# Soft-MoE slot work of three batches deferred to the last two head pairs, and chunk bounds from three products

## The chip, the core and the metric

The kernel runs on one core of a Trainium2 chip. The metric is the device time of one execution in microseconds (us). A core has five engines with queues of their own: TensorE (PE in the profile; PEld is its weight load), VectorE (DVE), ScalarE (ACT), GpSimd (POOL) and SyncE (SP). Each works off its own queue in the order in which the program wrote it; semaphores order the engines among each other. SBUF is the working memory, PSUM holds what TensorE writes. The loads are issued from GpSimd's queue, the stores from SyncE's.

## What is computed

Causal attention over selected key chunks, followed by a soft mixture of experts. Batch 4, heads 8, sequence 768, head dimension 64, key chunks of 32.

```python
# attention: each query keeps the 6 chunks with the largest upper bound
k_min, k_max = min and max of k over each chunk of 32 keys
ub = sum_d max(q * k_min, q * k_max)          # (B, H, S, 24), causal chunks only
sel = the 6 chunks of largest ub
scores = q k^T / 8, masked to sel and causal; attn = softmax(scores); x = attn v
# soft MoE on x as (3072, 512) with phi (512, 32), 8 experts of 4 slots, F = 1024
logits = x @ phi
d = softmax of logits over the 3072 rows      # dispatch, one column per slot
slot_input = d.T @ x                          # (32, 512)
slot_out[e] = relu(slot_input[e] @ w1[e]) @ w2[e]
c = softmax of logits over the 32 slots       # combine
out = c @ slot_out                            # (3072, 512)
```

## The kernel before

**Pairs.** The work runs over 16 pairs of heads, four per batch (pair 0 to 15; the text calls the loop step i "pair i"). Each step of the loop handles several pairs at different stages: the scores and exponentials of pair i, the bound and the search of pair i+1, the transposes of k and q of pair i+2, the products with v of pair i-1, the normalisation of pair i-2. Loads run four pairs ahead. The order of the work on each engine is the order in which the loop writes it; nothing reorders it.

**Scores.** `GROUPS` packs the causal blocks of a pair into six score groups of 384 or 512 columns. Each goes into one of two PSUM buffers (pool `p_sc`), is read by one ScalarE exponential (line 293, tile e_sb), and its diagonal blocks are cut by a GpSimd select (line 295). Between groups 1 and 2 the loop puts the bound products and the transposes of k, and the first half of the products with v; between groups 3 and 4 the transposes of q and more products with v.

**Bounds and search.** `evac_T` copies the transposed k and q to SBUF on ScalarE (line 190). `kmin` and `kmax` reduce k over chunks on VectorE, `qsplit` makes min(q,0) and max(q,0) (lines 215 and 216), and `ubound` forms the bound as min(q,0) k_min + max(q,0) k_max: one causal product (line 222) and twelve products of 128 x 48 (line 229). `select` runs twelve maximum-of-eight searches (line 241) and compares with the sixth largest (line 244). `ns_transposes` and `evac_ns` bring the result to the mask that is added to the scores.

**Slots.** When the four pairs of a batch are normalised and transposed, its slot work follows: `moe_logits` and `moe_copy` (copy and column maximum pm) at the end of the step i with i - 2 the last pair of the batch, that is i = 5, 9 and 13; and in the next step (6, 10 and 14) `moe_max`, `moe_bound`, `moe_exp` (running column maximum m_run, dispatch exponential d_sb, rescaling of the sum so far), `moe_comb` (row maximum, combine exponentials into the padded tile c_pad), `moe_dispatch` (30 small products into si, added to si_acc) and `moe_ct` (six transposes of c_pad and a copy into cT_all). The last batch does the same after the loop, in code of its own. The tag "tp" of pool `p_tp` has two PSUM buffers that all transposes, bounds and slot sums share.

**Experts.** After the loop: `experts_in` (x w1), `relu`, `hidden_T`, `experts_out` (w2), then 24 products with c and the stores. The 16 weight pieces of 1024 KB (pieces 0 to 7 are w1, 8 to 15 w2) are loaded along the loop. `EARLY` = 14 of them have tiles of their own; pieces 14 and 15 get theirs at the start of steps 14 and 15, in space that closed input pools leave. `wplan` says how many pieces a step issues:

```python
wplan = {i: 1 for i in range(-1, NPAIR)}
for i in (0, 1):
    wplan[i] = 0
```

`keep` issues idle products after the loop; their results are not used.

## Time and profile before

| | |
|---|---|
| device time, median of 3 runs | 173.73 us (173.69 to 173.76) |
| span of the profiled execution (first to last instruction) | 172.0 us; its device time is not listed apart, so the 1.7 us around the span are taken from the median |
| TensorE busy | 137.7 us (80%), 2574 products |
| VectorE busy | 126.0 us (73%), 429 instructions |
| ScalarE busy | 122.2 us (71%), 163 instructions |
| GpSimd busy | 99.7 us (58%), 192 instructions |
| on the chain that ended last | PE 37%, ACT 27%, DVE 17%, DMA 8%, issue 7% |
| loads through GpSimd's queue | 26.25 MB written to SBUF |
| stores | 6.29 MB |

The shares of busy time are averages over stages with different limits, so the page alone does not say what bounds. The chain that ended last is followed back from the last instruction, at each step to what released it. "issue" is time in which an engine waited for nothing that the profile shows. A row of the chain or of a timeline gives start, length, engine, tile or line, and how many instructions were merged. A row of the stages gives the stretch, its length, the busy time of PE, PEld, DVE, ACT and POOL with their instruction counts, the granted clock of TensorE, the DMA share and GB/s. A group row gives the line, engine, operation, out<-in, count, then busy us and mean ns of one, then the idle time ahead of it and who ended it.

### The profile page before, as it was taken

How to read it: one execution, taken by the hardware profiler on the slowest of the kernel's cores; microseconds unless marked ns; L12 is line 12 of the kernel's file. 1: busy time of each engine (PE TensorE's matmuls, PEld its weight loads, DVE VectorE, ACT ScalarE, POOL GpSimd, SP SyncE). 2: the span in 40 equal slices, each digit the busy share in tenths (PEclk: the TensorE clock that was granted, in tenths of full speed). 3: DMA queues.
4: the chain of work that ended last, by engine and by line, in shares of the span. 5: the costliest groups of instructions: out<-in, count | busy, mean ns of one | idle time of the engine just before them, and what ended most of it. 6: DMA issues, size and time to landing. Idle time of an engine off the chain costs nothing.

```text
span 172.0 us, 6181 instructions
## 1 busy us (share of the span) xinstructions
PE 137.7 (80%) x2574; PEld 99.3 (58%) x2575; DVE 126.0 (73%) x429; ACT 122.2 (71%) x163; POOL 99.7 (58%) x192
## 2 busy tenths in 40 slices
PE   0458988999999789999988899999697989896310
PEld 0345465776767658766675676676565854774200
DVE  3468768999999988999997989999843652156530
ACT  2355999999999679899977799998567621265430
POOL 7977759789878666889774678558253710000000
PEclk9999999999999999999999999999999999999955
DMA  3999999999999999999999999999999950019995
GB/s 46 169 145 188 184 213 187 130 159 210 171 203 194 210 198 206 198 205 201 204 202 200 206 197 209 195 211 198 202 210 213 215 107 0 4 37 402 403 406 221
DMA packets 40460, 32.94 MB, mean 191 GB/s; under 512 B 26352, under 2 KB 34544, under 8 KB 40432
## 3 DMA queue, kind: packets, MB, share of 16 engines
q0 software_dynamic: 38416, 26.25, 103.2%
q1 hardware_dynamic: 2016, 6.29, 9.3%
q8 instruction: 20, 0.33, 0.7%
q14 instruction: 8, 0.07, 0.1%
HBM read 52.49 MB, written 6.29 MB: 342 GB/s over the span
## 4 chain that ended last, share of the span: by engine, by line
PE 37%; ACT 27%; DVE 17%; DMA 8%; issue 7%; POOL 0%; ACTq 0%; DVEq 0%; POOLq 0%
ACT e_sb L293 20%; PE sc_ps L270 7%; DMA out_dram<-o_sb 6%; PE tr_ps L181 5%; PE at_ps L314 5%; PE sc_ps L280 4%; DVE x_sb L327 3%; PE h_ps L654 2%; PE so_ps L694 2%; DVE qpn L216 2%; PE ub_ps L229 2%; DMA k_in<-in_k_dram 2%; ACT kT L190 2%; DVE mm L199 2%; DVE mm L205 2%
## 5 line engine op out<-in xcount | busy, mean ns | idle before, releaser
L293 ACT ACTIVATE e_sb<-sc_ps 128x768 bf16<-128x768 f32 (+1 forms) x96 | 82.7, 927 | 7.0 <-PE sc_ps L280 6.5
L295 POOL TENSOR_SCALAR_AFFINE_SELECT e_sb<-e_sb 128x256 bf16<-128x256 bf16 x96 | 39.2, 415 | 25.6 <-ACT e_sb L293 25.3
L270 PE MATMUL sc_ps<-qT,kT 64*128 64x384 bf16 (+3 forms) x288 | 40.2, 297 | 6.6 <-ACT e_sb L293 6.5
L280 PE MATMUL sc_ps<-nsT,smask 64*128 64x384 bf16 (+2 forms) x320 | 38.7, 281 | 0.0
L314 PE MATMUL at_ps<-v_t,e_sb 128*128 128x65 bf16 x672 | 29.8, 194 | 1.8 <-DVE x_sb L327 1.6
L270 PEld LDWEIGHTS <-kT 64*128 64x128 bf16 x288 | 17.3, 95 | 18.3 <-issue 13.2
L314 PEld LDWEIGHTS <-e_sb 128*128 128x128 bf16 x672 | 25.2, 98 | 4.2 <-issue 1.5
L241 DVE MAX8 mx<-ub_ps 128x8 f32<-128x8 f32 (+1 forms) x192 | 17.0, 162 | 3.4 <-POOL e_sb L295 1.9
L280 PEld LDWEIGHTS <-smask 64*128 64x128 bf16 x320 | 16.7, 96 | 3.6 <-issue 0.6
L190 ACT COPY kT<-tr_ps 128x768 bf16<-128x768 bf16 x16 | 12.8, 798 | 8.2 <-PE tr_ps L181 7.1
L199 DVE TENSOR_REDUCE mm<-kT 128x24 bf16<-128x768 bf16 x16 | 15.1, 944 | 4.1 <-ACT kT L190 4.0
L134 POOL DMA_DIRECT2D v_t<-in_v_dram x16 | 16.6, 1041 | 2.0 <-PE ns_ps L252 1.3
L327 DVE TENSOR_TENSOR x_sb<-at_ps,inv 128x768 bf16<-128x768 f32 (+1 forms) x17 | 15.5, 910 | 0.6
L205 DVE TENSOR_REDUCE mm<-kT 128x24 bf16<-128x768 bf16 x16 | 15.1, 943 | 0.0
L190 ACT COPY qT<-tr_ps 128x768 bf16<-128x768 bf16 x16 | 12.9, 805 | 2.1 <-PE tr_ps L181 2.1
L181 PE MATMUL tr_ps<-ident,k_in 128*64 128x128 bf16 x192 | 9.4, 240 | 5.6 <-DMA k_in<-in_k_dram 4.8
L129 POOL DMA_DIRECT2D k_in<-in_k_dram x16 | 11.7, 729 | 1.5 <-POOLq L760 0.8
L740 ACT ACTIVATE o_sb<-o_ps,cinv 128x512 f32<-128x512 f32 x12 | 8.1, 686 | 5.6 <-DMA out_dram<-o_sb 4.3
L129 POOL DMA_DIRECT2D q_in<-in_q_dram x16 | 11.5, 720 | 0.0
L216 DVE TENSOR_SCALAR qpn<-qT 128x768 bf16<-128x768 bf16 x16 | 11.5, 716 | 0.0
L122 POOL DMA_DIRECT2D w_sb<-in_moe_w_dram x16 | 11.3, 708 | 0.0
L738 DVE TENSOR_SCALAR o_sb<-o_ps,cinv 128x512 f32<-128x512 f32 x11 | 8.0, 748 | 4.3 <-DMA out_dram<-o_sb 3.1
(116 smaller groups left out, 195.5 us busy)
## 6 DMA issues: line engine op xcount, KB each, us to landing
w_sb<-in_moe_w_dram POOLq DMA_DIRECT2D x16, 1024.0 KB, 13.4
out_dram<-o_sb SPq DMA_DIRECT2D x10, 512.0 KB, 5.4
k_in<-in_k_dram POOLq DMA_DIRECT2D x16, 192.0 KB, 9.6
q_in<-in_q_dram POOLq DMA_DIRECT2D x16, 192.0 KB, 9.6
v_t<-in_v_dram POOLq DMA_DIRECT2D x16, 192.0 KB, 10.1
out_dram<-o_sb SPq DMA_DIRECT2D x4, 256.0 KB, 3.3
phi_sb<-in_moe_phi_dram POOLq DMA_DIRECT2D x1, 32.0 KB, 8.8
```

Source lines behind the costliest of these rows:

```text
L129: nc.gpsimd.dma_start(out=t, in_=src.rearrange("h (p g) d -> p h (g d)", p=P))
L181: nc.tensor.matmul(ps[h * 64:(h + 1) * 64, g, :], lhsT=src[:, h, g * D:(g + 1) * D], rhs=ident, is_transpose=True,)
L190: nc.scalar.copy(t.rearrange("d (p g) -> d p g", g=NQT), st.pop((nm + "ps", i)).rearrange("d g p -> d p g"),)
L199: nc.vector.tensor_reduce(mm[:, 0, 0, :], kT, axis=AX.X, op=ALU.min)
L205: nc.vector.tensor_reduce(mm[:, 1, 0, :], kT, axis=AX.X, op=ALU.max)
L241: nc.vector.max(mx[:, a, :], ub[:, a, :max(8, 4 * t + 4)])
L270: nc.tensor.matmul(ps[:, h, c:c + w], lhsT=kT[r, kg * P:(kg + 1) * P], rhs=qT[r, qs], start=True, stop=False,)
L280: nc.tensor.matmul(ps[:, h, c + (f - t0) * P:c + (l - t0) * P], lhsT=smask[r, x, kg].rearrange("p a b -> p (a b)"), rhs=nsT[r, (f - x * NJ ...
L293: nc.scalar.activation(e[:, :, :w], st.pop(("scps", i, g))[:, :, :w], func=ACT.Exp, scale=scale)
L295: nc.gpsimd.affine_select(out=e[:, :, :P], in_=e[:, :, :P], compare_op=ALU.is_ge, fill=0.0, base=0, pattern=[[0, 2], [1, P]], channel_mult ...
L314: nc.tensor.matmul(o, lhsT=st["e", i, g][:, h, c:c + P], rhs=v_t[i % NV][:, h, kg, :], start=(kg == 0), stop=(kg == t),)
L327: nc.vector.tensor_tensor(st["x", b][:, t0:t1, 2 * j:2 * j + 2, :].rearrange("p t h d -> p h t d"), at[:, :, :, :D], inv.broadcast_to([P, ...
```

## The change

**Deferred slots.** Batches 0 to 2 do only the logits and the copy at i = 5, 9 and 13, into a tile lg_all that holds all three; their normalised x stays in SBUF (pool xo, three buffers). At the end of step 13 one reduction (`old_max`) takes the column maximum over the three batches. Step 14 does the transpose of that maximum, the shift, the exponential and the combine part for all 18 row blocks at once; step 15 and the code after the loop do the joint dispatch (18 products for each of five column groups) and the transposes of c.

**Bounds.** q is stored as -q, k_min as -k_min. The bound is (-q)(-k_min) + max(q,0)(k_max - k_min), by three products of the same shape in each row block: 18 for 12. The exponential takes the scale -1/8, and the mask changes its sign. `qsplit` is one VectorE instruction. Row block 0 has four chunks at most, so all are kept: it gets one maximum over four chunks and a threshold of -3e38 set once, and no search.

**Weights.** EARLY is 12. No piece is issued in steps 0, 1, 4 and 8, two in step 12. Pieces 12 to 15 are issued by `late_weight` once a pool closes: in step 13, in step 14 behind the search, after the loop, and behind the last products with v.

```diff
-    EARLY = 14
+    EARLY = 12
+    OLD = B - 1
+    NO = OLD * NQT
...
-        nc.scalar.copy(
+        nc.scalar.activation(
             t.rearrange("d (p g) -> d p g", g=NQT),
             st.pop((nm + "ps", i)).rearrange("d g p -> d p g"),
+            func=ACT.Copy, scale=-1.0 if nm == "q" else 1.0,
         )
...
-        nc.vector.tensor_scalar_min(t[:, 0, :], qT, 0.0)
-        nc.vector.tensor_scalar_max(t[:, 1, :], qT, 0.0)
+        nc.vector.tensor_scalar(t, st["qT", i], -1.0, 0.0, op0=ALU.mult, op1=ALU.max)
...
-            for x in range(2):
+            for z, (w, x) in enumerate(((qT, 0), (qp, 0), (qp, 1))):
                 nc.tensor.matmul(
-                    o, lhsT=qpn[:, x, t * P:(t + 1) * P],
-                    rhs=bd[:, x],
-                    start=False, stop=(t == NQT - 1 and x == 1),
+                    o, lhsT=w[:, t * P:(t + 1) * P], rhs=bd[:, x],
+                    start=False, stop=(t == NQT - 1 and z == 2),
                 )
...
+        nc.vector.tensor_reduce(mx[:, 0:3:2, 0:1], ub[:, 0:3:2, :4], axis=AX.X, op=ALU.max)
         for a in range(NQT * 2):
             t = a // 4 + NJ * (a % 2)
-            nc.vector.max(mx[:, a, :], ub[:, a, :max(8, 4 * t + 4)])
+            if t > 0:
+                nc.vector.max(mx[:, a, :], ub[:, a, :4 * t + 4])
...
     def moe_copy(b):
-        lg = small.tile([P, NQT, NS], F32, name="lg", tag="lg")
+        nc.vector.tensor_copy(lg_all[:, b], st.pop(("lgps", b)))
...
+    def old_max():
+        nc.vector.tensor_reduce(pm, lgo.rearrange("p n s -> p s n"), axis=AX.X, op=ALU.max)
+    def old_maxT():
+        nc.tensor.matmul(pmT, lhsT=st.pop("pm"), rhs=identf, is_transpose=True)
+    def old_bound():
+        nc.vector.tensor_reduce(mb, st.pop("pmT"), axis=AX.X, op=ALU.max)
+    def old_shift():
+        ... bc, m_run, ld = lgo - m_run over [P, NO, NS]
+    def old_exp():
+        nc.scalar.activation(d_o, st.pop("ld"), func=ACT.Exp)
+    def old_rows():
+        nc.vector.tensor_reduce(rm, lgo, axis=AX.X, op=ALU.max)
+        nc.vector.tensor_tensor(lgo, lgo, rm.broadcast_to([P, NO, NS]), op=ALU.subtract)
+    def old_comb():
+        ... two exponentials of lgo into c_pad [P, NO, 4, CH]
+    def old_dispatch(dgs):
+        ... 18 products for each dg of dgs; with the last dg a copy into si_acc
...
-    wplan = {i: 1 for i in range(-1, NPAIR)}
-    for i in (0, 1):
-        wplan[i] = 0
+    wplan = {i: 1 for i in (-1, 2, 3, 5, 6, 7, 9, 10, 11)}
+    wplan[12] = 2
```

In the loop (`LAST` is 15) the new calls stand at these places; behind each the engines that it uses:

```
step 13: ... moe_copy(2), old_max (DVE)
step 14: scores 0, 1 | old_maxT (PE) | ubound(15), normalise(12) | old_bound (DVE) | select(15) | late_weight
         pv(13) first half | old_shift (PE, DVE) | scores 2, 3 | old_exp (ACT) | x_transposes, evac_x | old_rows (DVE)
         scores 4, 5 | old_comb (ACT) | ns_transposes, evac_ns, rest of pv(13)
step 15: scores 0, 1 | moe_ct(0) (PE, DVE) | normalise(13) | pv(14) first half | old_dispatch([0]) (PE) | scores 2, 3
         x_transposes, pv(14) | old_dispatch([1, 2]) | scores 4, pv(14), scores 5
after:   late_weight | moe_ct(1) | old_dispatch([3, 4]), copy (DVE) | normalise(14), pv(15), x_transposes(14) ...
         moe_ct(2) with a ScalarE copy in the place of keep(2) | i_ctx.close(), late_weight | memsets, tail as before
```

More of the change, by code (lines that the diff above doesn't have):

```diff
@@ L84 @@
     cT_all = static.tile([P, B * NQT, P], BF16, name="cT_all")
-    c_pad = static.tile([P, NQT, 4, CH], BF16, name="c_pad")
+    c_pad = static.tile([P, NO, 4, CH], BF16, name="c_pad")
+    lg_all = static.tile([P, OLD, NQT, NS], F32, name="lg_all")
     si_acc = static.tile([P, NDG + 1, NS], F32, name="si_acc")
-    m_run = [static.tile([P, NS], F32, name=f"m_run{i}") for i in range(2)]
+    m_run = static.tile([P, NS], F32, name="m_run")
     w_sb = []
@@ L147 @@
     nc.vector.memset(ones_sq, 1.0)
+    for t in mx_t:
+        nc.vector.memset(t, -3e38)
     for t in v_t:
@@ L393, in moe_exp @@
         nc.vector.tensor_tensor(
[L394 removed]
+            ld, lgo, m_run.rearrange("p (o s) -> p o s", o=1).broadcast_to([P, NO, NS]), op=ALU.subtract,
         )
[L396 to L404 removed]
@@ L438, in moe_ct @@
+                    rhs=d_sb[:, k, :], start=(k == 0), stop=(k == n - 1),
+                )
+    def old_dispatch(dgs):
+        if 0 in dgs:
+            st["si_o"] = p_tp.tile([P, NDG + 1, NS], F32, name="si_ps", tag="tp")
+        dispatch(st["si_o"], st["d_o"], [(st["x", b], t) for b in range(OLD) for t in range(NQT)], dgs)
+        if NDG in dgs:
+            nc.vector.tensor_copy(si_acc, st.pop("si_o"))
+    def moe_ct(b, copy=nc.vector.tensor_copy):
         ps = p_tp.tile([P, NQT, P], BF16, name="cT_ps", tag="tp")
@@ L580 @@
     evac_x(LAST, 3, NQT)
-    keep(2)
+    moe_ct(2, nc.scalar.copy)
     moe_logits(BL, range(NDG - 1, NDG), lg1)
+    i_ctx.close()
+    late_weight()
+    pads = ctx.enter_context(tc.tile_pool(name="pads", bufs=1))
+    siT_pad = pads.tile([P, NDG, E, CH], BF16, name="siT_pad")
+    hT_pad = pads.tile([P, NFG, E, CH], BF16, name="hT_pad")
     nc.gpsimd.memset(siT_pad, 0.0)
     nc.gpsimd.memset(hT_pad, 0.0)
-    i_ctx.close()
     tail = ctx.enter_context(tc.tile_pool(name="tail", bufs=1))
-    m_old = m_run[(BL + 1) % 2]
+    m_old = m_run
     pm = small.tile([P, NS], F32, name="pm", tag="pm")
@@ L621 @@
     keep(1)
-    moe_dispatch(BL)
+    si = p_tp.tile([P, NDG + 1, NS], F32, name="si_ps", tag="tp")
+    dispatch(si, d_sb, [(st["x", BL], t) for t in range(NQT)], range(NDG + 1))
     op = ctx.enter_context(tc.tile_pool(name="op", bufs=5))
-    si = st.pop("si")
     zrow = tail.tile([1, 4, CH], F32, name="zrow")
```

158 lines of the change are left out of this document (71 added, 87 removed).

## Prediction

> **What bounds the kernel now.** I read the span and the DMA strip first, then the chain that ended last, then the busy time by stages, and last the timelines of TensorE and VectorE at the places that the chain names.
>
> ```profile
> core 0 of [0], span 172.0 us
> DMA  3999999999999999999999999999999950019995
> ```
>
> The sum below is made on this span. The median of the three runs is 173.73 us, so 1.7 us lie around the span; they are added at the end unchanged. The DMA engines are busy for the first 33 of 40 slices: the loads are a second bound that lies close behind the first, and they come back among the rivals.
>
> The chain, over one ordinary pair:
>
> ```profile
> 41.32 1.77 ACT e_sb L293 x2
> 43.86 0.30 PE ub_ps L229 x12
> 44.16 0.46 PE tr_ps L181 x12
> 44.61 0.48 PE at_ps L314 x12
> 45.10 0.32 PE sc_ps L270 x2
> 45.68 0.45 ACT e_sb L293
> ```
>
> An ordinary pair is one closed ring. ScalarE works off its exponentials; the last of them frees a score buffer; TensorE then does the second score group of the next pair, the bound products (ub_ps), the transposes of k, the first products with v and the third score group, in this order; and ScalarE goes on only when that group is done (45.68). VectorE and GpSimd do not appear. Whatever is added to TensorE between 43.1 and 45.7 lengthens every pair; whatever is taken from VectorE in an ordinary pair gains nothing.
>
> The stages, from the start of one third exponential to a later one (columns: stretch, its length, then the engines' busy times):
>
> ```profile
> 45.68:52.55 6.87, 6.55 (x132) 4.73 (x128) 6.46 (x23) 6.53 (x9) 5.75 (x12) 1.00 1.19 193
> 52.55:69.71 17.16, 15.26 (x321) 11.69 (x316) 15.40 (x54) 13.72 (x19) 11.62 (x22) 1.00 1.34 202
> 83.45:101.06 17.61, 15.34 (x321) 11.80 (x316) 15.56 (x56) 13.89 (x20) 11.66 (x23) 1.00 1.32 202
> 114.80:123.65 8.85, 8.09 (x163) 6.06 (x157) 8.06 (x29) 6.16 (x9) 5.06 (x10) 1.00 1.31 203
> 123.65:131.21 7.56, 5.12 (x111) 3.97 (x111) 3.86 (x9) 5.39 (x9) 3.10 (x7) 1.00 1.24 208
> 131.21:136.43 5.22, 5.01 (x111) 3.78 (x106) 2.41 (x5) 4.57 (x5) 2.43 (x5) 1.00 1.07 216
> ```
>
> An ordinary pair takes 6.87 us. The two pairs that carry the slot work of batch 0 take 17.16 us, 3.42 more than two ordinary ones; batch 1 costs 17.61 - 13.74 = 3.87. Batch 2 is in the fourth and fifth row. Only there is the slot work on the path, and there it is a relay of small VectorE, TensorE and ScalarE steps:
>
> ```profile
> 119.50 0.48 DVE pm L365
> 120.15 0.72 DVE x_sb L327
> 121.29 0.97 DVE mx L241 x12
> 122.28 0.46 DVE ns_t L244
> 122.87 0.37 DVE ld L393
> 123.75 1.83 ACT e_sb L293 x2
> ```
>
> The exponential of the slots (d_sb) stands in ScalarE's queue ahead of the third score group, so that group waits for ld behind the whole search. A pair later it goes on so:
>
> ```profile
> 126.82 0.74 PE si_ps L426 x30
> 127.56 0.40 PE at_ps L314 x12
> 127.96 0.35 PE cT_ps L440 x6
> 128.33 0.56 DVE cT_all L443
> 129.06 0.97 DVE x_sb L327
> 130.08 0.55 PE at_ps L314 x12
> ```
>
> Thirty products of the dispatch take 0.74 us, 25 ns each; six transposes of c and their copy to SBUF follow, and only then the normalisation (x_sb) that releases the products with v.
>
> **The change, part by part.**
>
> *Three bound products for two (adds).* Six more weight loads and products in each pair, between second and third score group, on the ring.
>
> ```profile
> 43.70 0.46 PE L229 MATMUL ub_ps<-bd,qpn 128*128 128x48 bf16 x12
> 44.09 0.53 PE L181 MATMUL tr_ps<-ident,k_in 128*64 128x128 bf16 x12
> ```
>
> Twelve go from 43.70 to 44.09, that is 33 ns each; six more cost 0.20 us. Thirteen such passes lie ahead of the third exponential of pair 13 (114.80): 13 x 0.20 = +2.5 us. Nothing hides it. Lower bound: the 25 ns of the narrower dispatch products, +1.9; upper bound within the ring: the 12 transposes at 0.46/12 = 38 ns, +3.0. I take 33, which is the same operation. The Trainium skill (TensorE: Matmul & The Clock Gate, Back-to-back issue gap) speaks against this part: it gives about 81 ns as the sustained spacing of weight load and product at 128 columns. By that the thirteen passes would cost 6.3 us and the sum would end at +2.2 us; the trace's 33 ns for 48 columns do not agree with it.
>
> *q split, search and copies (removes, mostly free).* One VectorE pass makes max(q,0) where two made min and max; one small maximum over four chunks replaces two searches of row block 0; k and q are evacuated by an activation with a scale in the place of a copy, of the same size on the same engine. In ordinary pairs VectorE is off the ring: nothing. At the start it is on it:
>
> ```profile
> 8.92 0.79 DVE qpn L216
> ```
> ```profile
> 15.80 0.62 PE ub_ps L229 x11
> ```
>
> The first pair waits 0.79 us for the second pass of the split, and this one goes. But the products run slower there (0.62/11 = 56 ns), so two passes of six more cost 0.67 of it back where they are exposed, and behind the split the smask copy on ScalarE is next. I take -0.3 us, between -0.8 and +0.3. The longer memset of the padded c tile lies before the first k arrives.
>
> *Batches 0 and 1 (moves).* Pairs 5, 6, 9 and 10 keep only the logits and one copy on VectorE:
>
> ```profile
> 55.97 0.75 PE L356 MATMUL lg_ps<-phi_sb,xT_sb 128*128 128x32 bf16 x24
> ```
>
> These 0.75 us fall mostly into TensorE's wait for the last exponential; the copy fits into VectorE, which is freed of the second split pass and of pm. So of 3.42 + 3.87 = 7.29 us I leave 0.2 per batch: -6.9. Bounds: nothing left (-7.3), or the logits and a copy fully exposed, 1.0 a batch (-5.3).
>
> *Window of pair 13 to 14.* The joint maximum runs over 576 values where pm ran over 192. VectorE's price per element is (0.97 - 0.40)/576 = 1.0 ns, from x_sb (768 values, above) and lc (192):
>
> ```profile
> L412 DVE TENSOR_TENSOR lc<-lg,rm 128x192 f32<-128x192 f32 x3 | 1.2, 396 | 0.1
> L397 ACT ACTIVATE d_sb<-ld 128x192 bf16<-128x192 f32 x3 | 1.1, 363 | 4.2 <-DVE ld L393 4.2
> L393 DVE TENSOR_TENSOR ld<-lg,m_run 128x192 f32<-128x192 f32 x3 | 1.1, 357 | 0.1
> L410 DVE TENSOR_REDUCE rm<-lg 128x6 f32<-128x192 f32 x3 | 1.0, 346 | 0.0
> ```
> ```profile
> L415 ACT ACTIVATE c_pad<-lc 128x96 bf16<-128x96 f32 x6 | 1.4, 278 | 1.3 <-DVE lc L412 1.3
> ```
>
> So the maximum takes 0.48 + 0.38 = 0.86, and normalise behind it ends 0.2 to 0.4 us later than at 121.1 (120.15 + 0.97), the lower if the shorter q split lets it begin earlier. But the joint exponential is queued behind the third and fourth score groups, so these no longer wait for search and ld: 121.3 + 0.48 (products with v) + 0.3 (the broadcast, an estimate at the size of the 0.35 for six transposes) + 0.6 (scores) = 122.7, where it was 123.7. I take -0.85; from -1.4 (maximum hidden) to +0.4 (the broadcast waits for VectorE's queue).
>
> *Window of pair 14 to 15.* ScalarE gets 0.36 + 0.34 = 0.70 for the joint exponential (0.9 ns an element from the two activations above) and 0.9 for two of 288 in the place of 0.46; ld, row maxima and their subtraction are 0.74, 0.73 and 0.78 on VectorE beside it. Of what followed on the path (126.82 to 130.08), the 30 products leave (-0.74); the transposes of batch 0 and their copy take the place of batch 2's, but now wait for the c exponentials; 18 products of the joint dispatch (25 ns each, 0.45) stand ahead of the third score group. Sum +0.70 + 0.44 + 0.45 - 0.74 = +0.85, and 0.15 for the wait: +1.0, from +0.3 to +1.8.
>
> *From there to the last logits.* TensorE is busy 5.01 of 5.22 us, so what is added counts: 36 products ahead of the fifth score group, 0.90; transposes of batch 1, 0.37; 36 more products, 0.90; and now normalise of pair 14 stands in VectorE's queue behind the copy of their sum (0.35) instead of beside the scores, of which I count 0.4 more. Sum +2.9; from +1.5 (products fill waits) to +4.4 (both c copies and the sum's copy in series). Batch 2's transposes replace the two idle keep products: nothing. The late weights are cover that may go, below.
>
> Sum: +2.5 - 0.3 - 6.9 - 0.85 + 1.0 + 2.9 = -1.65 us. Span 170.4, time **172.1 us**.
>
> **The rivals.**
>
> *The join costs more (slower).* Place: pairs 14, 15 and the end, where hardly an engine has slack. With the upper bounds of the last three terms (+0.4, +1.8, +4.4) the sum is +1.9, 175.6 us; it turns slower once the three exceed the 4.7 us that the other terms save. For it: three steps are single-file through VectorE and the one bound buffer of the joint sum. Against it: before, VectorE was busy only 2.41 of 5.22 us there. Middle of the part of this case that is slower: 174.8.
>
> *The join hides (faster).* Lower bounds of the last two terms (+0.3, +1.5): -3.75, 170.0 us. For it: ScalarE and VectorE idle in 123.65 to 131.21. Against it: the DVE queue's order is fixed.
>
> *The last weight piece comes late.* It is now issued only when the last products with v are done. These with v end where the sixth row of the stages ends, 136.43; less the 1.65 of the sum it is issued near 134.8. It is needed by the products at
>
> ```profile
> 147.97 1.89 PE so_ps L694 x64
> ```
>
> shifted to 146.3. So 11.5 us are left:
>
> ```profile
> DMA to landing us min/median/max: 9.4/13.4/18.3
> ```
>
> At the median it stalls 1.9 us (174.0, no difference that can be told); slower from 13.6 us on; at the maximum 178.9. Against it: only one other piece is ahead in the queue by then, so I expect the minimum, 144.2.
>
> *The deferral doesn't free the pairs.* If logits, copy and their buffer are the excess, 1.0 a batch stays: 173.7.
>
> *Products at the early spacing of 56 ns.* At six times 56 ns, 0.34 a pair, the thirteen passes cost 4.4 in the place of 2.5: +0.25, 174.0, and any dearer is slower. Only the first pairs show this spacing. By the spacing that the Trainium skill gives (TensorE: Matmul & The Clock Gate, Back-to-back issue gap) it would be 175.9.
>
> **How the numbers follow.** A measurement of this kernel tells 0.2%, 0.35 us, from no change. Forecast 0.57 (172.1; own range 170.8 to 173.3); join hides 0.12; join costs more 0.13; late weight 0.08 (0.03 same, 0.05 slower); not freed 0.06 (0.04 same, 0.02 slower); products dearer 0.04 (slower). Faster: 0.54 + 0.12 = 0.66. Same: 0.03 (the upper end of the forecast) + 0.03 + 0.04 = 0.10. Slower: 0.13 + 0.05 + 0.02 + 0.04 = 0.24. The range 170.0 to 174.8 takes the hiding join and the middle of the costly one in; the late weight at its worst and the costlier half of the join stay out.
>
> **What would show it.** Ordinary pairs at 7.07 us with 18 bound products in 0.6 us; VectorE's share of an ordinary pair down by 0.6 or more; pairs 5, 6, 9 and 10 within 0.3 us of the ordinary ones; the third exponential of pair 13 near 110; the first logits of the last batch near 134.8; no wait of the expert products for a DMA. Ordinary pairs above 7.2 us, more than 4 us added after pair 13, or so_ps waiting for a weight load would prove it wrong.

## The result, and the profile after

| | before | after |
|---|---|---|
| device time, median | 173.74 us | 172.26 us (172.09 to 173.58) |
| ratio, 95% interval | | 0.994 (0.9917 to 0.9963) |
| profiled execution: time, span | span 172.0 us | 173.2 us, span 171.5 us |
| VectorE busy in the span | 126.0 us, 429 instructions | 114.9 us, 380 instructions |
| TensorE products | 2574 | 2663 |

The change gains 0.6% (1 - 0.994; the ratio is taken over all single times, the quotient of the two medians is 0.9915). 172.1 us was forecast. One thing is needed to read the numbers: the times of the changed kernel lie in two groups, 172.1 to 172.3 us with a mean granted TensorE clock of 0.961 to 0.970, and 173.2 to 173.6 us with 0.953 to 0.955, and the profiled execution is one of the second group.

```profile
core 0: 171.5 us, clock 0.954
```

The stages of the changed kernel, cut as in the prediction (stretch, length, busy PE, PEld, DVE, ACT, POOL with counts, granted clock, DMA share, GB/s): an ordinary pair, the pairs of batch 0 and of batch 1, the window of pair 13 to 14, that of pair 14 to 15, and from there to the last batch's first logits.

```profile
37.92:44.95 7.03, 6.71 (x138) 4.89 (x134) 5.83 (x22) 6.54 (x9) 5.82 (x12) 1.00 1.22 191
51.96:66.12 14.16, 13.83 (x294) 10.39 (x290) 11.96 (x43) 13.02 (x17) 11.63 (x23) 1.00 1.41 175
80.16:94.31 14.15, 13.82 (x294) 10.38 (x289) 12.26 (x43) 13.01 (x17) 11.48 (x23) 1.00 1.44 191
108.35:116.72 8.37, 7.21 (x153) 5.54 (x149) 7.37 (x25) 5.77 (x7) 4.51 (x10) 1.00 1.27 209
116.72:125.60 8.88, 6.36 (x119) 4.47 (x115) 4.88 (x10) 6.19 (x10) 2.93 (x7) 0.97 1.27 206
125.60:134.83 9.23, 8.17 (x185) 6.68 (x181) 3.35 (x8) 4.57 (x5) 2.34 (x5) 0.84 0.78 138
```

The slot work has left the middle: two pairs with a batch in them take 14.16 us, 0.10 more than two ordinary ones (14.06), where they took 17.16 and 17.61. It has come back in the last two rows, which grew from 7.56 and 5.22 to 8.88 and 9.23 us. In the last row the granted clock is 0.84; before it was 1.00.

Pair 0's third exponential starts at 16.87 us (before 18.21). Between the two profiles (after less before) the stretches differ so:

| stretch | predicted | measured |
|---|---|---|
| start, to pair 0's third exponential | -0.3 | -1.34 |
| pair 0 to 13: thirteen bound passes, and batches 0 and 1 deferred | +2.5 - 6.9 = -4.4 | 91.48 - 96.59 = -5.11 |
| window 13 to 14 | -0.85 | -0.48 |
| window 14 to 15 | +1.0 | +1.32 |
| to the last batch's first logits | +2.9 | +4.01 |
| logits to the experts' last products with w2 (so_ps x64) | 0 | +0.07 |
| these products to the end (so_ps x64 at 147.97 before, 146.44 after) | 0 | 25.06 - 24.03 = +1.03 |
| sum | -1.65 | -0.50 |

Of the difference of 1.15 us to the forecast, the first two rows bring 1.75 us more gain than predicted and the others 2.90 us more cost. The two largest costs without a term are the clock in the sixth stage and the stretch after the experts, where the change edits nothing. The table compares an execution of the second group. Those of the first have spans of 170.4 to 170.5 us, that is -1.5 to -1.6 in all, but no profile shows their stages.

### The profile page after: what moved, and what is told of

It is laid out like the page before. It is cut to its first block, busy times and chain, and to the rows that moved or that the text cites. A ratio compares the mean times of both kernels' runs of the same rounds, so it can differ in the third digit from the quotient of the medians.

```text
span 171.5 us, 6310 instructions
## 1 busy us (share of the span) xinstructions
PE 139.8 (82%) x2663; PEld 101.4 (59%) x2663; DVE 114.9 (67%) x380; ACT 122.0 (71%) x156; POOL 99.1 (58%) x192
## 4 chain that ended last, share of the span: by engine, by line
PE 38%; ACT 24%; DVE 21%; DMA 7%; issue 5%; SPq 1%; DVEq 0%; ACTq 0%; POOLq 0%
ACT e_sb L300 19%; PE sc_ps L277 6%; DMA out_dram<-o_sb 5%; DVE mm L207 5%; PE at_ps L321 5%; DVE mx_t L248 4%; PE ub_ps L235 4%; PE sc_ps L287 4%; PE tr_ps L188 3%; DVE x_sb L334 3%; DVE ns_t L251 2%; PE h_ps L672 2%; PE so_ps L712 2%; DMA k_in<-in_k_dram 2%; PE si_ps L424 2%
## 5 line engine op out<-in xcount | busy, mean ns | idle before, releaser
L302 POOL TENSOR_SCALAR_AFFINE_SELECT e_sb<-e_sb 128x256 bf16<-128x256 bf16 x96 | 38.7, 416 | 24.9 <-ACT e_sb L300 24.4
L197 ACT ACTIVATE kT<-tr_ps 128x768 bf16<-128x768 bf16 x16 | 13.0, 810 | 7.9 <-PE tr_ps L188 7.8
L334 DVE TENSOR_TENSOR x_sb<-at_ps,inv 128x768 bf16<-128x768 f32 (+1 forms) x17 | 15.5, 910 | 0.6
L197 ACT ACTIVATE qT<-tr_ps 128x768 bf16<-128x768 bf16 x16 | 13.1, 818 | 2.4 <-PE tr_ps L188 2.4
L248 DVE MAX8 mx_t<-ub_ps 128x8 f32<-128x16 f32 (+4 forms) x160 | 14.5, 162 | 0.1
L751 PE MATMUL o_ps<-so_sb,cT_all 128*128 128x256 bf16 x48 | 8.0, 299 | 4.7 <-DVE o_sb L756 4.2
```

Of the source, the lines that this page charges most:

```text
L197: nc.scalar.activation(t.rearrange("d (p g) -> d p g", g=NQT), st.pop((nm + "ps", i)).rearrange("d g p -> d p g"), func=ACT.Copy, scale=-1 ...
L248: nc.vector.max(mx[:, a, :], ub[:, a, :4 * t + 4])
L302: nc.gpsimd.affine_select(out=e[:, :, :P], in_=e[:, :, :P], compare_op=ALU.is_ge, fill=0.0, base=0, pattern=[[0, 2], [1, P]], channel_mult ...
L334: nc.vector.tensor_tensor(st["x", b][:, t0:t1, 2 * j:2 * j + 2, :].rearrange("p t h d -> p h t d"), at[:, :, :, :D], inv.broadcast_to([P, ...
```

## The experiments

All times are medians, with the 95% interval of the ratio to the kernel before (173.80 to 174.03 us beside them). The ratio is taken over the single times, some of them near 176 us for the kernel before, and is not the quotient of the medians (for e0 that is 0.997). Each fence shows the difference from the kernel named in its heading.

| | us | ratio |
|---|---|---|
| e0, the changed kernel again | 173.36 | 0.9933 (0.989 to 0.9975) |
| e1, bounds alone | 175.28 | 1.0065 (1.0032 to 1.0099) |
| e2, deferral and weight plan alone | 171.58 | 0.9849 (0.9795 to 0.9904) |
| e3, after, cT of batch 0 later | 170.63 | 0.9800 (0.9747 to 0.9854) |
| e4, after, warm gap | 171.96 | 0.9888 (0.9858 to 0.9918) |
| e5, e3 with the fetch shifted | 170.06 | 0.9767 (0.9727 to 0.9807) |
| e6, e2 with the later cT | 169.02 | 0.9722 (0.9699 to 0.9745) |
| e7, after, v loads later | 173.16 | 0.9941 (0.9919 to 0.9962) |
| e8, e6 with the shorter search | 169.46 | 0.9736 (0.9705 to 0.9766) |
| e9, after, warm gap and fetch shifted | 171.16 | 0.9844 (0.9822 to 0.9867) |
| e10, e6 with idle products at the start | 168.35 | 0.9659 (0.9625 to 0.9693) |
| e11, e3 with idle products at the start | 168.49 | 0.9685 (0.9651 to 0.9719) |

### e0: the changed kernel again

No edit. 

> The changed kernel again. Its nine times so far lie in two heaps, 172.1 to 172.3 and 173.2 to 173.6 us. Theory D: the upper heap has one output DMA engine that lags at the end (20 to 30 GB/s for 1.2 us in the profile shown). Theory C: the upper heap has TensorE at half clock between 125 and 128 us. A profile whose time is in the lower heap shows full clock there under C, and no tail of 20 to 30 GB/s under D.

Measured: 173.36 us (171.95 to 174.21), 1.1 us over the first median of the same kernel. The profiled execution is the slowest of the twelve. It has both the half clock (0.59 in the stretch from 124 to 128 us) and the slow end of the stores, so it does not decide between the two theories. In this profile pair 0's third exponential comes at 18.05 us, not 16.87. Two things differ. The timelines of VectorE and GpSimd near 8.5 us, first of the changed kernel, then of its repetition:

```profile
8.40 1.05 POOL L139 DMA_DIRECT2D v_t<-in_v_dram  x1
8.46 0.35 DVE L222 TENSOR_SCALAR qp<-qT 128x768 bf16<-128x768 bf16 x1
```
```profile
8.41 2.07 POOL L139 DMA_DIRECT2D v_t<-in_v_dram  x2
8.79 0.82 DVE L222 TENSOR_SCALAR qp<-qT 128x768 bf16<-128x768 bf16 x1
```

The first k arrived 0.34 us later (transposes at 5.03 for 4.69). The same pass over q takes 0.35 us when it starts 0.06 us after the issue of the v loads, and 0.82 us when it starts 0.4 us after it. So it is at pair 0 in every profile that has this issue: a pass takes 0.35 us when it starts up to 0.2 us after the start of the issue, and 0.80 to 0.89 us from 0.3 to 0.4 us after it. And TensorE is slower: the two score products of 512 columns ahead of the exponential take 0.61 us here and in the kernel before, 0.39 in the changed kernel's profile. e10 comes back to this.

### e1: the kernel before, with the bounds part alone

```diff
-            for x in range(2):
-                    o, lhsT=qpn[:, x, ...], rhs=bd[:, x],
+            for z, (w, x) in enumerate(((qT, 0), (qp, 0), (qp, 1))):
+                    o, lhsT=w[...], rhs=bd[:, x],
...
```

> The kernel before with the bounds part alone (three products, one split pass, ten searches, -q), no deferral, no new weight plan. Theory A (each pass of 18 products costs 0.15 us on the ring, and the first pairs win 1.2 us by the shorter split and search): ordinary pairs 7.02 us, third exponential of pair 0 near 17.0 us, the two slot pairs of batch 0 and 1 about 0.5 us shorter each against ordinary ones; sum +2.2 - 1.2 - 1.0 to -0.5, so 173.7 to 174.3 us. Rival B (the early gain comes from the weights or the deferral): third exponential of pair 0 near 18.2 and 175.5 us.

Measured: 175.28 us, slower than before and over the expected 173.7 to 174.3. An ordinary pair, and the two pairs of batch 0 and of batch 1, in its stages:

```profile
44.90:51.91 7.01, 6.69 (x138) 4.87 (x133) 5.73 (x22) 6.53 (x8) 5.73 (x12) 1.00 1.24 207
51.91:68.87 16.96, 15.52 (x333) 11.92 (x329) 14.55 (x51) 13.86 (x19) 11.73 (x23) 1.00 1.35 202
82.91:100.68 17.77, 15.65 (x333) 12.04 (x329) 14.59 (x53) 13.93 (x21) 11.66 (x23) 1.00 1.33 202
```

The ordinary pair is 7.01 us, as in the changed kernel (7.03): the three products cost 0.15 us a pair and VectorE's shorter work (5.73 us for 6.46) gives nothing back there. Where slot work is on the path it does: 16.96 - 14.02 = 2.94 us for batch 0 against 3.42 before, and 17.77 - 14.02 = 3.75 us for batch 1 against 3.87. Pair 0's third exponential is at 16.82, pair 15's at 130.98 (before 131.21): the part is even over the loop. It loses 0.9 us from so_ps x64 to the end (172.7 - 147.74 = 24.96, before 24.03), where its DMA view looks like that of the changed kernel in e5: two packets of the instruction queue, and a slow end. Another 0.3 us lie around the span (174.77 - 172.7 = 2.1 us in the profiled execution, 1.7 in the other kernels); no run shows why.

### e2: the changed kernel, with the bounds of before

The reverse of e1's edit. 

> The changed kernel with the bounds of before (two products, two split passes, twelve searches, copies), so deferral and weight plan alone. Theory A: ordinary pairs 6.87 us, third exponential of pair 0 near 18.2, so 172.2 + 1.2 - 1.95 + 0.2 = 171.7 us (171.3 to 172.2). Rival B (the deferral needs the VectorE time that the bounds free): pairs 5, 6, 9 and 10 stay 0.5 us above ordinary ones and the time is 172.7 us or more.

Measured: 171.58 us. The deferral with its weight plan, which no run separates from it, gains 1.5% (1 - 0.9849) where the whole change gains 0.6%. Stages: ordinary pair, batch 0, batch 1, and the window of pair 14 to 15.

```profile
45.86:52.73 6.87, 6.55 (x132) 4.73 (x128) 6.46 (x23) 6.53 (x8) 5.13 (x11) 1.00 1.27 205
52.73:66.58 13.85, 13.52 (x282) 10.08 (x278) 13.18 (x46) 13.00 (x17) 11.71 (x23) 1.00 1.43 185
80.31:94.33 14.02, 13.58 (x282) 10.07 (x278) 13.51 (x46) 12.99 (x16) 11.40 (x22) 1.00 1.44 195
116.54:125.88 9.34, 6.82 (x119) 4.77 (x115) 4.88 (x10) 6.18 (x9) 3.10 (x7) 0.89 1.25 207
```

The deferred batches leave 13.85 - 13.74 = 0.11 us and 14.02 - 13.74 = 0.28 us; 0.2 each was forecast. The last row shows that this profile, too, has the lower clock at the end of the loop.

### e3: the changed kernel, cT of batch 0 later

```diff
-        if i == LAST:
-            moe_ct(0)
...
             old_dispatch([1, 2])
+            moe_ct(0)
```

> The changed kernel with the transposes of c of batch 0 moved from the start of pair 15 to behind the second part of the joint dispatch. Theory A (at the start of pair 15 they hold back the normalisation of pair 13 in VectorE's queue, TensorE idles 1.8 us): the third exponential of pair 15 comes 2.4 us earlier against that of pair 14, 0.4 is given back by the transposes: 170.2 us, and no half clock between 116 and 132 us. Rival (ScalarE's joint exponentials set pair 15): no difference, 172.2 us or 0.4 more.

Measured: 170.63 us, 2.0% under before. To see why, first the chain that ended last in the changed kernel, in pair 15 (start, length, what):

```profile
121.04 0.47 ACT c_pad L414
121.56 0.52 PE cT_ps L440 x6
122.11 0.56 DVE cT_all L441
122.84 0.97 DVE x_sb L334
123.85 0.55 PE at_ps L321 x12
124.41 0.44 PE si_ps L424 x18
124.85 0.32 PE sc_ps L277 x2
```

The transposes of c need the joint c exponentials on ScalarE; their copy stands in VectorE's queue ahead of normalise (x_sb); and TensorE cannot begin the products with v before x_sb has freed their one buffer. So TensorE does next to nothing from 122.07 to 123.85. The same window with the later cT, in the stages of e3:

```profile
117.83:124.31 6.48, 5.68 (x113) 4.09 (x109) 4.41 (x9) 6.19 (x10) 2.75 (x7) 1.00 1.33 202
124.31:132.70 8.39, 7.33 (x191) 6.08 (x183) 3.91 (x9) 4.57 (x5) 2.52 (x6) 1.00 1.04 204
```

6.48 us for 8.88, and the clock stays at 1.00. Only the place of these six transposes and their copy differs, so it costs the 2.40 us (0.18 of them through the clock, as e4 shows). Of this, 0.35 us come back in the next window, where the transposes now stand: 8.39 us for the 8.04 that e4 takes there at full clock.

### e4: the changed kernel, with TensorE kept busy in that gap

```diff
+        if i == LAST:
+            wm = p_tp.tile([P, 512], F32, name="wm_ps", tag="tp")
+            for _ in range(6):
+                nc.tensor.matmul(wm, lhsT=ident, rhs=w_sb[0][:, :512], ...)
         if have(i - 1):
             pv(i - 1, [0, 1, 2])
```

> The changed kernel with six idle products of 128x512 ahead of the last pair's first weighted sums, where TensorE stood idle from 122.0 to 123.85 us (their result is not used). Theory: the half clock granted from 125.0 to 128.3 us is caused by that idle stretch, and it is what made the stretch from the third exp of pair 15 (window 8.88) and the run to the last batch's logits (9.23) longer than predicted. Then the granted clock stays 1.00 there, the at_ps sums (1.20 us for 18) and si_ps products (1.11 for 36) shrink to about 0.7 and 0.8, and the last batch's first logits come about 1 us earlier (near 133.8 when pair 0's third exp is at 16.9): 171.2 us where the changed kernel has 172.3. Rival: VectorE's chain (cT copy, x_sb, si_acc, x_sb, xT) sets the end of that stretch and the clock costs nothing: logits unmoved, 172.3.

First the changed kernel in stretches of 1 us: TensorE is busy 0.07 and 0.15, and 1.2 us later the granted clock is at a half for 3 us.

```profile
122.00:123.00 1.00, 0.07 (x2) 0.00 (x0) 0.86 (x3) 0.90 (x2) 0.43 (x2) 1.00 1.16 221
123.00:124.00 1.00, 0.15 (x5) 0.15 (x6) 0.80 (x1) 0.00 (x0) 0.38 (x1) 1.00 1.05 213
125.00:126.00 1.00, 1.00 (x14) 0.55 (x10) 0.00 (x0) 0.40 (x1) 0.00 (x0) 0.54 1.00 201
126.00:127.00 1.00, 1.00 (x11) 0.66 (x8) 0.00 (x0) 1.00 (x2) 0.31 (x1) 0.50 1.10 221
127.00:128.00 1.00, 1.00 (x21) 1.00 (x20) 0.56 (x1) 0.54 (x1) 0.49 (x2) 0.50 1.07 217
```

With the idle products, the two last windows of e4:

```profile
116.49:125.19 8.70, 7.48 (x125) 4.89 (x120) 4.87 (x10) 6.18 (x9) 2.93 (x7) 1.00 1.27 208
125.19:133.23 8.04, 6.99 (x184) 5.80 (x178) 3.34 (x8) 4.57 (x5) 2.34 (x5) 1.00 0.90 161
```

The clock is 1.00 throughout, and the windows are 0.18 and 1.19 us shorter, 1.37 in all. The gap itself is still there; only the clock behind it is repaired. The rival (VectorE's chain sets the stretch) falls. The median, 171.96 us, is 0.3 us under the first median of the changed kernel and 1.4 under e0's, and over the expected 171.2. That executions of the lower group are those without the dip would fit, but it is not shown: none of them was profiled, and the mean clock does not tell, as e4's profile has 0.957 with full clock in these windows.

The Trainium skill (TensorE: Matmul & The Clock Gate, HAM oscillation) asks for no idle gap of more than about 3.4 us on TensorE. Here a gap of 1.8 us was followed by the half clock in this profile, so the length of the gap alone does not protect; the measurement decides.

### e5: e3 with 96 idle instructions at the start

```diff
+    fp = p_tp.tile([P, 8], F32, name="fp_ps", tag="tp")
+    for _ in range(48):
+        nc.tensor.matmul(fp, lhsT=ones_sq, rhs=ones_sq[:, :8], ...)
     for i in range(-2, NPAIR):
```

> The kernel of e3_ct_late (cT of batch 0 behind the old dispatch) with 48 idle products of 128x8 at the very start, while TensorE waits for the first k. Nothing else differs; the 96 more instructions only shift where in TensorE's stream each 16-KB instruction fetch falls. Theory: the fetch that fell about 4 us into the output stores now falls ahead of them, the stores' last 1.1 us at 20 to 30 GB/s go, and the stretch from the last products of the experts (so_ps x64) to the end shrinks from 25.0 to about 24.0 us: 169.6 us against 170.6. Rival: the slow end of the stores has another cause (the order of the stores, the y rows): 25.0 stays, 170.6.

The view is that of the DMA engines from the experts' last products to the end. First the changed kernel (146.4 to 171.5 us), then e5 (144 to 167.7 us); each window is cut into 40 equal slices.

```profile
GB/s 0 0 26 0 0 0 0 0 0 0 225 375 424 398 405 392 418 392 366 418 385 418 385 418 418 411 418 405 398 418 411 385 405 388 379 157 23 20 0 0
q8 instruction: 2, 0.03, 0.5%
```
```profile
GB/s 0 0 0 0 0 0 28 0 0 0 0 377 373 432 401 394 415 408 394 394 436 380 415 415 394 415 401 401 394 415 387 429 401 401 408 373 384 183 0 0
q8 instruction: 1, 0.02, 0.3%
```

In the changed kernel two packets of the instruction queue fall into this window, one before the stores and one among them (between 156 and 158 us), and the stores end with two slices (1.3 us) at about 20 GB/s: all but a small rest has landed, and the end waits for that rest. 400 GB/s over 16 engines are 25 GB/s for one, so by this estimate a single engine is still writing. In e5 one packet falls there, ahead of the stores, and the stores run at full rate to their end. One such packet holds an engine for about 1 us (0.5% of 16 engines over 25.1 us is 2.0 us for two). From so_ps x64 (144.05 in e5, 146.44 after, 144.31 in e3) to the end it is 23.65 us, where the changed kernel has 25.06 and e3 has 24.99. The median, 170.06 us, is 0.57 under e3's, less than the 1.34 of the two profiles; the ranges overlap (168.85 to 170.7, and 170.03 to 171.14).

The other profiles agree. From so_ps x64 to the end it is 24.96 to 25.06 us in the six in which such a packet falls among the stores (the changed kernel, e0, e1, e3, e4, e7), and 23.63 to 23.70 in e2, e5, e6, e9 and e11, where the last one falls ahead of them. With the bounds of before (e2) it falls ahead, with the bounds alone (e1) among the stores: the cost at the end comes with the three products, by where their instructions move the fetch.

The bounds part adds 96 products (six in each of 16 pairs) with their weight loads to TensorE's instructions; that moves the fetches along the kernel, and this one happens to fall into the stores. The Trainium skill (Runtime: NRT & Kernel Launch, Instruction fetch mechanics) says that instructions are fetched in blocks of 16 KiB, 256 of them, at a cost that is mostly hidden. The size agrees with the page of the changed kernel,

```profile
q8 instruction: 21, 0.34, 0.7%
```

0.34 MB in 21 packets; hidden it is only where no store is late by it.

### e6: e2 with the later cT

Both edits from above: bounds of before, and cT of batch 0 behind `old_dispatch([1, 2])`. 

> The deferral alone, with the bounds of before (two products, two VectorE passes, a search over all row blocks), and the cT of batch 0 behind the old dispatch. Theory: the two parts add up: e2_deferral's 171.58 less the 2.1 us that the later cT brought in the last pair (less some 0.3 us if VectorE, which has 0.4 us more to do per pair in this form, is late there), and no instruction fetch among the stores: 169.5 to 169.9 us, ordinary pairs 6.87. Rival: in this form VectorE is the later engine in the last pairs, so the move brings less: 170.5 or more.

Measured: 169.02 us (168.86 to 169.61), 2.8% under before. The parts add: the later cT brings 2.6 us here, from e2's 171.58. Ordinary pairs 6.87, pair 15's third exponential at 122.99. The profiled execution, the slowest of the four, has half clock from 131 to 134 us, behind three stretches of 1 us in which TensorE is busy 0.60, 0.65 and 0.46. Of the kernels without idle products none has a lower median.

### e7: the changed kernel, v loads of pairs 0 and 1 later

```diff
-    load_v(0)
-    load_v(1)
...
         if i == -1:
+            load_v(0)
+            load_v(1)
             nc.gpsimd.dma_start(out=phi_sb, ...)
```

> The changed kernel with the loads of v for pairs 0 and 1 issued behind pair 0's search instead of ahead of it. Theory: the one pass of VectorE over q takes 0.28 us when GpSimd is quiet and 0.76 to 0.89 when GpSimd is issuing the v loads, and which of the two happens (the first k lands at 3.3 or at 3.7 us after its issue) makes the two groups of times 172.1 and 173.3. Then qp takes about 0.3 us, pair 0's third exp comes at 16.9 to 17.1, and the times lie together near 172.2. Rival: the pass is slow for another reason, or the v loads now collide with the search of pair 1: pair 0's third exp at 17.4 or later, times spread as before.

The theory fell. Pair 0's pass over q took 0.35 us, but the times lie in the same two groups (172.32 to 172.50, and 173.16 to 173.50), and pair 0's third exponential is at 17.40. Its score products of 512 columns still take 0.61 us (at 16.32), so the pass was not what made the start late here. What goes with the groups is the mean clock: the higher one has mean clocks of 0.954 to 0.960 and the lower of 0.962 to 0.970, and this profile, of the higher group, has the half clock from 124 to 127 us.

### e8: e6 with the shorter search

```diff
+        nc.vector.tensor_reduce(mx[:, 0:3:2, 0:1], ub[:, 0:3:2, :4], axis=AX.X, op=ALU.max)
...
-            nc.vector.max(mx[:, a, :], ub[:, a, :max(8, 4 * t + 4)])
+            if t > 0:
+                nc.vector.max(mx[:, a, :], ub[:, a, :4 * t + 4])
```

> The kernel of e6_late_old (deferral, two products, two passes over q, later cT) with one piece of the bounds part added: row block 0 without its search (one reduce in place of two). Theory: what the bounds part gains is gained at the start alone and most of it comes from the one pass over q in place of two; the shorter search is worth 0.2 to 0.5 us there (pair 0's third exp near 18.0 where e6_late_old has 18.37) and nothing in the ordinary pairs, which TensorE sets (6.87): 168.7 to 169.0 us against 169.0. Rival: the search is the greater part of the 1.34 us that the profile of the changed kernel gained at the start: third exp near 17.3, 168.1 us.

Pair 0's third exponential comes at 18.11 us for 18.37, but 0.20 of this is there when the search begins (10.38 for 10.58; k arrived earlier). From the search to the comparison behind it pass 1.02 us for 1.09: it is worth 0.07, less than expected, and the rival is out. The median, 169.46 us (168.47 to 170.16), cannot be told from e6's. The chain that ended last shows where an earlier loop no longer helps:

```profile
131.87 11.98 DMA w_sb<-in_moe_w_dram
143.89 1.92 PE so_ps L712 x61
```

The last weight piece is issued at 131.87, lands 11.98 us later, and the products with w2 wait 0.5 us for it. This is the prediction's rival of the late weight piece, come true where the piece is issued 3.2 us earlier than in the changed kernel (135.1) and lands as late as 11.98 us after its issue; why it takes so long is not shown. In e11 a piece issued at 131.97 is waited for by no product.

### e9: both unforeseen costs taken away from the changed kernel

e4's six idle products and 42 of e5's at the start, 96 instructions together. 

> The changed kernel with both of the unforeseen costs taken away: six idle products in the last pair's gap (as in e4_warm) and 42 small ones at the start, 96 instructions more in all, which move the instruction fetch ahead of the stores. Theory: the two are separate and add up: clock 1.00 at 125 to 129 us, 23.7 us from the experts' last products to the end where the changed kernel has 25.1, a profiled span of about 168.7 us where the changed kernel had 171.5, and a median near 170.6. Rival: with the dip gone the fetch falls elsewhere or the stores are late for another reason: over 24.5 us in the store phase, median 171.9 as in e4_warm.

Measured: span 169.1 us (after 171.5), time 171.16 us (170.87 to 171.6, one group). The clock is 1.00 in the last windows, and 23.63 us pass from so_ps x64 (145.47) to the end. In the profile the two add up; the span is 0.4 over the expected 168.7, as much as pair 0's third exponential is later than in the changed kernel's profile (17.28 for 16.87). The median is 0.5 over the expected 170.6.

### e10: e6 with TensorE busy at the start

```diff
+    wu = p_at.tile([P, 2, 512], F32, name="wu_ps", tag="at")
+    def warm(n):
+        for _ in range(n):
+            nc.tensor.matmul(wu[:, 0, :], lhsT=ones_sq, rhs=<512 zeros of c_pad>, ...)
+    warm(3)                                  # before the loop
...
+        if i == 0:
+            warm(3)                          # in ubound, behind the causal product
...
         if i == -1:
+            warm(2)
             ns_transposes(0)
```

> e6_late_old (bounds of before, deferral, later cT) with eight idle products of 128x512 in TensorE's waits at the start: three before the first k, three before pair 0's bound products, two before its mask transposes. Theory: at the start TensorE runs at half speed (two score products of 512 columns take 0.61 us, later 0.39) until a moment that differs from execution to execution, near 19.9 us in e6_late_old and near 15.5 in the changed kernel's profile, and that moment, not VectorE's shorter work, is the greater part of the 1.34 us; work on TensorE brings it forward. Then those products take 0.39 us, pair 0's third exponential comes at 17.0 to 17.5 us instead of 18.37, and the time is 168.0 us (167.7 to 168.3), with less spread. Rival: the speed at the start is not TensorE's clock or does not hang on its work: 0.61 stays, third exponential at 18.2 or later, 169.0 us.

The score products of 512 columns ahead of pair 0's third exponential, in TensorE's timeline of e6 and of e10:

```profile
17.30 0.61 PE L276 MATMUL sc_ps<-qT,kT 64*128 64x512 bf16 x2
```
```profile
16.57 0.39 PE L278 MATMUL sc_ps<-qT,kT 64*128 64x512 bf16 x2
```

The third exponential comes at 17.38 us (18.37 in e6). Part of the gain is an earlier k (bound's first pass at 8.49 for 8.78). The speed itself rose as expected; the column of the granted clock says 1.00 in all these stretches and does not show it. By the durations, full speed is reached at 15.3 to 18.9 us in the eight profiles above with three products, at 19.6 to 21.5 in the four with two (in e6 two products of 384 columns take 0.53 us at 20.20 and 0.34 at 21.79, so the expected 19.9 was too early), and by 15.7 in e10. So work on TensorE seems to bring it forward, on one profile of each kernel, and the changed kernel's 1.34 us contain it. But the profile pays it back: in the next pair TensorE is busy 0.48 and 0.58, and the clock drops.

```profile
20.00:21.00 1.00, 0.48 (x7) 0.35 (x8) 0.88 (x3) 1.00 (x3) 1.00 (x2) 1.00 1.30 217
21.00:22.00 1.00, 0.58 (x8) 0.32 (x6) 0.70 (x2) 1.00 (x2) 0.76 (x3) 0.88 1.23 223
22.00:23.00 1.00, 1.00 (x18) 0.69 (x14) 0.00 (x0) 0.82 (x2) 0.53 (x2) 0.50 1.05 210
```

Pair 0 to pair 1 takes 8.25 us in place of 6.87. The profiled execution is the slowest of e10's (169.69; the median is 168.35, the fastest 167.42), and its end waits for the last weight piece too (issued at 132.05, landed 12.20 later, so_ps at 144.29).

### e11: the same with the bounds of the changed kernel

e3 with the five later products of e10, and 43 products of 128x8 in the place of the first three. 

> The same with the bounds of the changed kernel: e3_ct_late with five idle products of 128x512 in the two later places and 43 small ones before the first k, which also shift the instruction fetch ahead of the stores. With warm start, no gap and no fetch among the stores in both, the difference to e10_warm_start is the bounds part alone. Theory: it is a loss: 0.15 us a pair over 13 to 15 pairs, +2.0 to +2.2, less 0.5 to 0.8 at the start (one pass and a shorter search, twice), so 1.2 to 1.7 us slower than e10_warm_start: near 169.4 us. Rival: with TensorE warm the shorter VectorE work brings the start forward by more than 1.5 us and the bounds part is even: 168.0 us.

Measured: 168.49 us (168.18 to 169.68), which e10's 168.35 cannot be told from. In the profiles e11 has pair 0's third exponential at 17.00 and pair 15's at 123.30, that is 106.30 later; e10 has 17.38 and 123.38 less the 1.38 of its dip, 104.62 later. So in the loop the three products cost 1.68 us over 15 pairs, near the theory; e3 and e6, without idle products, give 106.33 - 104.62 = 1.71. Less 0.38 at the start, 1.3; but e11 itself has half clock from 12 to 15.5 us, ahead of that exponential, so the 0.38 is not clean. Further on, e10 waits 0.7 us for the weight piece and e11 does not (so_ps x64 at 143.30), so the medians do not show it. Neither of the two forecasts of the median (169.4, 168.0) came out, and this pair of kernels does not settle what the bounds part is worth when nothing else binds.

## Why the prediction was right, and where it was not

**Three products: +1.95, not +2.5.** The ring was read rightly, the price was mis-sized. The changed kernel's TensorE timeline, the first and last group of three:

```profile
49.83 0.19 PE L235 MATMUL ub_ps<-bd,qT 128*128 128x48 bf16 x1
...
50.21 0.18 PE L235 MATMUL ub_ps<-bd,qT 128*128 128x48 bf16 x1
```

Fifteen products in 0.38 us are 25 ns each. The 33 ns had divided by twelve a stretch that held, besides twelve products, the change to the transposes. The lower bound (25 ns) was the value. The 81 ns that the prediction weighed from the Trainium skill (TensorE: Matmul & The Clock Gate, Back-to-back issue gap) are not seen; e1 and the changed kernel both show 0.15 us a pair.

**Start: -1.34 in one profile, -0.16 in the other, not -0.3.** Step by step in the profile: k arrived 0.11 us earlier; the one pass for two gives 0.54 (the search of pair 0 starts at 9.77 for 10.42, that is 0.65); search and pair 1's shorter pass give 0.31 (pair 1's search, below, first before, then after, is 0.96 earlier); and the score products at full speed give the remaining 0.38.

```profile
16.46 1.06 DVE L241 MAX8 mx<-ub_ps 128x8 f32<-128x8 f32 x12 [0.72 <-PE ub_ps L229]
```
```profile
15.50 0.17 DVE L244 TENSOR_REDUCE mx_t<-ub_ps 128x2 f32<-128x8 f32 x1 [0.96 <-PE ub_ps L235]
```

The step that failed: the 0.67 us that the twelve dearer products were to pay back did not come, and pair 1's shorter pass was not counted. That the remaining pass can meet GpSimd's issue (e0), and that the spacing of 56 ns was a TensorE at lower speed and not a price of these products, was not seen.

**Batches 0 and 1: -7.06, forecast -6.9.** Right: -5.11 less the thirteen passes; e2 shows 0.11 and 0.28 left by the two batches, 0.39 where 0.4 was forecast. The rival that deferral frees nothing is out.

**Window 13 to 14: -0.48, forecast -0.85.** Inside its bounds. The joint maximum was costed at 0.86 us; in VectorE's timeline it takes 1.13:

```profile
112.96 1.13 DVE L376 TENSOR_REDUCE pm<-lg_all 128x32 f32<-128x576 f32 x1
```

**Window 14 to 15: +1.32, forecast +1.0; to the logits: +4.01, forecast +2.9.** With the clock repaired (e4) they are 8.70 - 7.56 = +1.14 and 8.04 - 5.22 = +2.82, within 0.15 us of the forecast. The work was counted rightly; the clock was not a term. But the wait of 0.15 us for the c exponentials was the wrong item inside a right sum: e3 shows that the place of these transposes and their copy alone costs 2.40 us in the window. Without them it takes 6.48 us, 1.08 less than before. The prediction's other items come to about zero (1.0 less the 0.15, less the 0.35 + 0.56 of batch 2's transposes and copy that it let batch 0's replace). So two errors of about 1 us cancel: the sum of this window was right by luck.

**The end: +1.03, forecast 0.** No term. e5 and e9 show its cause, the instruction fetch among the stores.

**Rivals.** The last weight piece did not come late in the changed kernel. It is issued at 135.1, landings after the issue are

```profile
DMA to landing us min/median/max: 8.6/11.4/16.0
```

and no product with w2 waits for a load. It comes late in e8 and e10, whose loops are faster: the condition was right, and the changed kernel only kept clear of it. The costly join nearly happened: its three terms came to -0.48 + 1.32 + 4.01 = 4.85 us in the profile, over the 4.7 at which the prediction put the turn of the sign; the sign held because the other terms saved 1.34 + 5.11 = 6.45. Without the dip they are 3.48, with 3.05 forecast. So one of the signs that the prediction named for being wrong, more than 4 us added after pair 13, did come up in this profile; 1.37 of the 4.85 are the clock, and the rest is within 0.5 us of the three terms. The hiding join did not happen, nor did products at 56 ns.

So the median agreed to 0.2 us, but the agreement is partly luck: costs and gains that were not forecast nearly cancel, and the median belongs to the executions of the lower group. The repetition (e0) has its median in the upper one, at 173.36 us, 1.3 over the forecast; in both the kernel is under the one before.

## What to carry to other kernels

Moving serial work to one place pays only when the queue at that place is ordered for it: six transposes and one copy put behind the normalisation that TensorE waits for doubled the gain of the deferral (2.3 us in e2, 4.8 in e6). Price an added product by the spacing between its own neighbours in the timeline, never by a stretch that holds the change to the next kind. When a stretch grows that no edit touches, look at the granted clock and at the packets of the instruction queue before looking at the code.

## What was not expected of the hardware

- A TensorE gap of 1.8 us (busy 0.07 and 0.15 in two stretches of 1 us) was followed by about 3 us of half clock, which cost 1.37 us; in e10 two stretches of half load (0.48, 0.58) and in e6 three (0.60, 0.65, 0.46) were followed by it as well. All three profiles of the changed kernel's order without idle products (the first, e0, e7) have it; whether its other executions do is not shown.
- At the start TensorE runs at a lower speed until some moment between 15 and 21.5 us that differs between executions (512 columns: 0.61 us for two products, then 0.39), and the granted clock does not show it.
- One 16-KB instruction fetch among stores that run at 400 GB/s goes with an end that is 1.3 to 1.4 us later, in six profiles of six; 96 instructions more or less decide whether it falls there. Which store it holds up, and why the others cannot make up for it, the profile does not show.
- A VectorE pass over 128x768 bf16 takes 0.35 us, and 0.80 to 0.89 when it starts 0.3 to 0.4 us into GpSimd's issue of the v loads.
- The times of e0, e5, e8, e10 and e11 range over 1.5 to 2.3 us. The clock and the landing of the last weight piece are candidates; which of them it is in the executions without a profile stays open.
